# One attention-and-FFN kernel, its commands split into single loads, casts and masks and put in another order

## The chip, the cores and the metric

One core of a Trainium2 chip. The metric is device microseconds of one execution; lower is better. The kernel has 3 runs: 200.95 us median, 199.65 to 203.45. The engines are TensorE (PE in the profile, its weight loads PEld), VectorE (DVE), ScalarE (ACT), GpSimd (POOL) and SyncE (SP, which only issues transfers here). Each runs its own instructions strictly in the order in which the program gives them, and waits for the others by semaphores.

## The reference

Attention over 4 batches, 8 heads, 768 positions, 64 wide, then a maxout FFN on the 3072 tokens:

```python
scores = scale * np.matmul(q, k.transpose(0, 1, 3, 2))
stream_keep = causal & (is_sink | in_win)          # sinks 4, window 64
mask = np.where(retrieval_head, causal, stream_keep)
a = softmax(np.where(mask, scores, -1e9))
x = np.matmul(a, v)            # -> [3072, 512]
h = np.maximum(np.maximum(x @ w1, x @ w2), x @ w3)
out = h @ w_out                # 512 -> 768 -> 512
```

A head is a retrieval head (all of the causal part) or a streaming head (a window and the sinks); which it is comes as data.

## The kernel before

**Units of work.** A batch has two halves of 384 queries. The first half sees 3 key blocks of 128, the second half 6. Heads go in quads of four, that is in two pairs of two heads. An index t counts batch, half and quad: t = 0, 1 are the two quads of batch 0's first half, 2 and 3 of its second half, 4 and 5 of batch 1's first half, up to 15. "Pair 0 to 3" of batch 0 are its four pairs of heads; the first half's third pair is pair 2.

**The steps.** Scores are computed transposed, keys on the partitions: `s t u` (L553) multiplies keys and queries into PSUM for part u of quad t (two parts in a first half, four in a second), and ACT takes the exponential into `pt` (L564). `k t i u e` multiplies a part of `pt` of pair i by a 0/1 mask on engine e (L586). `av t i` multiplies `pt` by the values with a column of ones (L602); DVE takes the reciprocal and scales (L610, L612) into `x`. `x` is turned by a transposing DMA (`av ... D`, L621) or by PE and a copy (`x t i`, L634, L638) into `xT`. Values are cast to f16 into `va` (L504) and, multiplied by a flag of the head, into `vf` (L506); `v t i` does both, one behind the other.

**The FFN.** When a half has its four `xT`, its FFN is put on a queue. Each command `f 1 e` computes one more block of it: one of 18 blocks of four matmuls (L438, 128x384 out of 512), where the first of three is copied out by engine e (L455) and the others are reduced by a maximum on DVE (L458, into `acc` and `hT`), and then three output blocks of six matmuls (L474, copied by engine e, L480). An output block takes two commands, the second of which does nothing. In batch 0's first FFN all blocks of one weight matrix come first, then those of the next.

**Batch 0's queries and keys.** They come by plain DMA in f32 (`hl half pair n`, L187), from SP, keys and queries of n pairs together; are cast to f16 (`cast half pair`, L212, one engine for keys and one for queries); and are turned by six PE transposes and copied into `KQ` (`turnp`, L231, L239). In batch 0's first half the mask is added on PE before the exponential (L537). Later batches come by a casting DMA from POOL (`load b qd`, L251) and are turned on DVE by stream transposes (`turn`, L267). Values come from SP (`load_v b half`, L287), weights by casting DMAs from POOL (`w`, L403, L410).

**What sets the order.** `PROGRAM`, a hand-kept list of 480 commands, is executed in order when the program is built; each command appends its instructions to the engines' queues. No scheduler moves anything. `idle n` issues n matmuls of zeros (L322). Buffers: two score tiles `st` in PSUM, four PSUM banks for all else, five `pt`, three f16 casts each of keys and queries, three value tiles. The letters a, d, p at the end of a command name ACT, DVE and POOL; with two letters, one for each of two instructions.

Of the kernel before, what the change touches and what calls it, by code (L numbers as in the profile page):

```python
# [10 lines left out]
FP16 = mybir.dt.float16  # L11
# [32 lines left out]
FIRST = "hl 0 0 1, ir"  # L44

PROGRAM = (
    "idle 2, idle 8, cast 0 0 aa, hl 0 1 1 ss, hl 0 2 2 ss, read, hl 1 0 2 ss, cast 0 1 pp",
    "flags, cast 0 2 ap, em 1, turnp 0 1 a, far, em 0, turnp 0 0 aa, cast 0 3 da, em 2, em 3",
    "load_v 0 0 4 4, s 0 0 1, s 0 0 0, v 1 1 pp, cast 1 1 pa, turnp 0 3 dd, turnp 0 2 da",
    "w 0 2 0, load_v 0 0 0 4, v 0 0 dp, s 1 0 0, w 0 2 1, s 0 1 0 b, hl 1 2 2 ss, s 1 0 1",  # L50
    "cast 1 2 dp, v 1 0 dd, s 0 1 1, s 1 1 0 b, av 0 0, v 0 1 pp, turnp 1 1 a, s 1 1 1",
    "turnp 1 2 aa, x 0 0 a, s 2 0 1, cast 1 0 dp, load_v 0 1, cast 1 3 ad, av 1 1, s 2 1 1",
    "av 1 0, x 1 1 d, av 0 1, turnp 1 0 ad, s 2 2 1, x 1 0 d, s 3 0 0, m 0, w 1, x 0 1 d",
    "s 2 0 0, m 3, m 1, f 1 d, f 1 d, s 2 1 0, s 2 2 0, m 2, f 1 a, f 1 d, k 2 1 2 p, k 2 0 1 d",
    "w 2, f 1 d, s 2 3 1, load 1 0, w 3, k 3 0 0 d, s 3 1 0, f 1 a, s 2 3 0, load 1 1",
    "k 2 0 3 p, k 2 0 2 p, turnp 1 3 dd, k 3 0 1 p, k 2 1 1 d, k 2 1 3 d, f 1 d, f 1 d",
    "v 2 0 ad, f 1 a, f 1 a, v 3 1 pp, f 1 d, s 3 0 1, v 2 1 dp, s 3 1 1, f 1 a, v 3 0 ap",
    "av 2 0 D, f 1 d, f 1 d, s 3 2 0, turn 1 0 0 0, turn 1 0 0 1, f 1 a, turn 1 0 1 0, s 3 2 1",
    "s 3 3 0, k 3 0 2 p, k 3 1 2 p, turn 1 0 1 1, f 1 a, av 2 1 D, s 3 3 1, k 3 1 1 d",
    "k 3 0 3 p, k 3 1 3 p, f 1 a, k 3 1 0 d, load_v 1 0, gate, f 1 a, s 4 0, k 4 1 0 p",  # L60
    "v 4 0 pp, av 3 0, av 3 1, f 1 a, f 1 a, x 3 0 d, s 4 1, turn 1 1 0 1, x 3 1 a, f 1 d",
    "v 5 1 pp, turn 1 1 1 0, turn 1 1 1 1, turn 1 1 0 0, k 4 0 1 d, k 4 0 0 d, k 4 1 1 p, f 1 a",
    "f 1 a, f 1 d, load_v 1 1, f 1 a, f 1 a, f 1 a, v 4 1 pd, f 1 a, f 1 d, s 5 0, f 1 a, f 1 d",
    "av 4 0 D, k 5 0 0 d, f 1 d, s 5 1, k 5 0 1 p, load_v 2 0, f 1 a, f 1 a, load 2 0, f 1 a",
    "s 6 0, f 1 d, av 4 1 D, f 1 a, v 5 0 ap, f 1 a, s 6 1, f 1 a, av 5 0 D, f 1 d, f 1 d",
    "k 5 1 1 p, k 5 1 0 p, v 7 0 dp, s 6 2, k 6 1 2 p, f 1 a, av 5 1 D, turn 2 0 1 0, f 1 a",
    "v 6 0 ad, s 6 3, turn 2 0 0 1, x 5 1 d, f 1 a, turn 2 0 1 1, load 2 1, load 3 1",
# [12 lines left out]
    "k 10 0 2 p, v 11 1 ap, av 10 0 D, f 1 d, s 11 2, k 11 0 2 p, turn 3 0 0 0, f 1 a",  # L80
    "turn 3 0 0 1, f 1 d, k 11 0 1 d, f 1 a, k 10 1 2 d, f 1 d, v 10 1 ap, f 1 a, turn 3 1 0 1",
    "f 1 a, f 1 a, s 12 0, av 10 1 D, f 1 a, f 1 d, k 12 1 0 p, s 12 1, f 1 d, f 1 a, f 1 a",
    "k 12 0 1 p, turn 3 1 0 0, s 11 3, v 12 1 ad, f 1 a, load_v 3 1, f 1 a, f 1 a, k 11 0 3 d",
    "k 11 1 3 p, f 1 d, f 1 d, k 11 1 1 p, turn 3 1 1 1, f 1 a, f 1 d, av 11 0 D, f 1 d",
    "k 11 1 2 d, f 1 a, k 12 0 0 p, k 12 1 1 d, f 1 a, s 13 0, av 12 0 D, f 1 d, av 11 1 D",
    "k 13 0 0 d, f 1 d, f 1 d, s 13 1, f 1 d, v 15 1 pp, f 1 d, k 13 0 1 p, x 11 1 d, f 1 d",
    "v 15 0 ad, av 12 1 D, k 13 1 1 d, av 13 0 D, s 15 0, f 1 a, f 1 d, f 1 d, f 1 a, f 1 d",
    "f 1 d, f 1 a, k 13 1 0 d, s 15 1, v 14 0 ap, f 1 d, f 1 a, f 1 d, f 1 d, s 14 0, f 1 a",
    "f 1 d, f 1 d, f 1 d, av 13 1 D, s 14 1, f 1 d, x 13 1 d, f 1 d, f 1 d, f 1 a, f 1 a",
    "s 14 2, f 1 a, k 14 1 2 p, v 14 1 ad, k 14 1 1 p, f 1 d, f 1 d, f 1 d, f 1 a, f 1 a",  # L90
    "k 15 0 1 p, s 14 3, f 1 d, k 14 0 3 p, f 1 a, f 1 d, s 15 2, f 1 a, f 1 d, f 1 d, f 1 d",
    "s 15 3, f 1 a, k 15 1 1 d, f 1 a, k 15 1 3 d, f 1 a, k 15 1 2 d, k 14 0 1 p, f 1 a",
    "k 14 0 2 p, k 14 1 3 p, k 15 0 3 d, av 14 0 D, f 1 a, f 1 a, f 1 a, av 14 1 D, f 1 a",
    "f 1 d, k 15 0 2 p, av 15 1 D, f 1 a, av 15 0 D, f 1 d, x 15 1 d, f 1 a, f 1 d, f 1 a",
    "f 1 d, f 1 d, f 1 a, f 1 a, f 1 a, f 1 d, f 1 a, f 1 a, f 1 d, f 1 d, f 1 a, f 1 d, f 1 a",
    "f 1 a, f 1 a, f 1 a, f 1 a, f 1 d, f 1 a, f 1 d, f 1 a, f 1 d, f 1 a, f 1 d, f 1 a, f 1 a",
# [13 lines left out]
def kernel(  # L110
# [68 lines left out]
    def load_pairs(half, hp, n, engines):  # L179
        for nm, src, eng in zip(("ks", "qs"), (k, q), engines):  # L180
            st = (
                pairs2.tile([P, 4, HB, D], FP32, tag=nm, name=nm) if n == 2
                else once.tile([P, 2 * n, HB, D], FP32, name=f"{nm}{hp}")
            )
            m = 2 * n if eng is nc.gpsimd else 2
            for h in range(0, 2 * n, m):
                eng.dma_start(  # L187
                    out=st[:, h : h + m],
                    in_=src[
                        0, 2 * hp + h : 2 * hp + h + m, half * HALF : (half + 1) * HALF  # L190
                    ].rearrange("h (p j) d -> p h j d", p=P),
                )
            for i in range(n):
                staged.setdefault((half, hp + i), []).append(st[:, 2 * i : 2 * i + 2])

    def load_cast(half, hp, n):
        for nm, src in (("kc", k), ("qc", q)):
            st = half16.tile([P, 4, HB, D], FP16, tag=nm, name=nm)
            nc.gpsimd.dma_start(
                out=st[:, 0 : 2 * n],  # L200
                in_=src[
                    0, 2 * hp : 2 * hp + 2 * n, half * HALF : (half + 1) * HALF
                ].rearrange("h (p j) d -> p h j d", p=P),
            )
            for i in range(n):
                cast.setdefault((half, hp + i), []).append(st[:, 2 * i : 2 * i + 2])

    def cast_pair(half, hp, engines):
        cast[half, hp] = []
        for nm, src, op in zip(("kn", "qn"), staged.pop((half, hp)), engines):  # L210
            x = half16.tile([P, HB, 2, D], FP16, tag=nm, name=nm)
            op(out=x, in_=src.rearrange("p h j d -> p j h d"))  # L212
            cast[half, hp].append(x)
# [6 lines left out]
    def turn_pair(half, hp, *engines):  # L220
        if (0, hp // 2) not in KQs:
            KQs[0, hp // 2] = qkt.tile([P, 2, S, 2], FP16, tag="KQ", name="KQ")
        xs = cast.pop((half, hp))
        n = 2 // len(engines)
        for part, op in enumerate(engines):
            tr = bank([P, 1024], FP16, "tr")
            for i in range(n):
                for j in range(HB):
                    c, x = i * HALF + j * P, xs[part + i]
                    if x.shape[1] == HB:  # L230
                        nc.tensor.transpose(  # L231
                            tr[:, c : c + P], x[:, j].rearrange("p h d -> p (h d)"), ident
                        )
# [65 lines left out]
    def load_first(half, hp, n, e="sc"):  # L299
        by = {"s": nc.sync, "c": nc.scalar}  # L300
        load_pairs(half, hp, n, [by[x] for x in e])
# [414 lines left out]
```

## Time and profile before

| | |
|---|---|
| runs shown | 200.95 median, 199.65 to 203.45 us |
| span of the profiled execution | 199.9 us (no other time of it is shown; the median is 1.05 above) |
| PE busy | 190.0 us, 95% |
| DVE busy | 148.3 us, 311 instructions |
| ACT busy | 115.9 us, 171 instructions |
| POOL busy | 90.5 us, 118 instructions |
| first exponential, first FFN product, first output product | 9.85, 23.64, 45.9 us |
| last matmul ends | 196.7 us |

The mean granted clock of TensorE is 0.990; it is 0.50 to 0.72 from 8 to 12 us and 1.00 afterwards. A stretch row of the profile gives, for a window of the span, the busy time of each engine; a busy PE is not the same as a needed PE, since ends of matmuls are modelled. A timeline row gives start, duration, engine, line, operation, and in brackets how long the engine had been idle and what ended that. Durations of neighbours on one engine overlap, so the sum of durations is more than the busy time.

### The profile page before, as it was taken

What the parts mean: (1) busy time and instruction counts of PE and PEld (TensorE: products, weight loads), DVE (VectorE), ACT (ScalarE), POOL (GpSimd) and SP (SyncE); (2) the same over time, 40 slices, a digit from 0 to 9 for tenths busy, and PEclk for the clock granted to TensorE, in tenths of its full rate; (3) what the DMA queues carried; (4) which work ended last, traced back from release to release, by engine and by line L of the source; (5) the groups of instructions that cost most, each with busy time, mean ns of one, the idle gap of its engine ahead of it and who ended that gap; (6) DMA issues with size and microseconds to landing.
All of it is one profiled execution on the core that took longest, in us unless ns stands there. A gap on an engine that the chain in (4) does not pass through costs nothing.

```text
span 199.9 us, 5135 instructions
## 1 busy us (share of the span) xinstructions
PE 190.0 (95%) x2059; PEld 109.3 (55%) x2059; DVE 148.3 (74%) x311; ACT 115.9 (58%) x171; POOL 90.5 (45%) x118
## 2 busy tenths in 40 slices
PE   7688898999999999999999999999999999999993
PEld 2345444565556455666456645574656455765552
DVE  3638965998976789896469998996978288767750
ACT  4489983765658798687776756634366565100011
POOL 3429187583276598490697245652010197000000
PEclk9889999999999999999999999999999999999999
DMA  5999999995979989988521232703500120124004
GB/s 143 312 245 230 196 195 212 208 169 76 283 173 211 162 169 208 218 218 176 147 76 23 43 124 74 159 20 73 167 5 20 53 108 0 23 59 157 3 0 157
DMA packets 48429, 26.48 MB, mean 132 GB/s; under 512 B 36758, under 2 KB 43926, under 8 KB 48406
## 3 DMA queue, kind: packets, MB, share of 16 engines
q1 hardware_dynamic: 43366, 17.96, 37.9%
q0 software_dynamic: 4624, 7.87, 21.9%
q8 instruction: 16, 0.26, 0.6%
q10 hardware_dynamic: 416, 0.33, 0.5%
q14 instruction: 7, 0.06, 0.1%
HBM read 25.17 MB, written 6.29 MB: 157 GB/s over the span
## 4 chain that ended last, share of the span: by engine, by line
PE 75%; DMA 11%; DVE 4%; SPq 3%; issue 2%; ACT 2%; POOL 0%; DVEq 0%
PE yy L438 39%; PE yy L474 14%; PE st L553 9%; PE oacc L602 9%; DMA vs<-in_v_dram 7%; PE yst L438 3%; DMA qs<-in_q_dram 2%; DVE KQ L267 2%; SPq L187 2%; ACT pt L564 1%; DMA xT<-x 1%; PE yst L474 1%; DVE acc L458 1%; DVE hT L458 1%; SPq L621 1%
## 5 line engine op out<-in xcount | busy, mean ns | idle before, releaser
L564 ACT ACTIVATE pt<-st 128x1024 f16<-128x1024 f32 (+3 forms) x98 | 83.3, 905 | 33.0 <-PE st L553 31.0
L586 POOL TENSOR_TENSOR pt<-pt,mk 128x512 f16<-128x512 f16 (+1 forms) x54 | 57.3, 1088 | 38.4 <-ACT pt L564 20.1
L438 PE MATMUL yy<-xT,w1t 128*128 128x384 f16 x180 | 35.8, 327 | 1.2 <-DVE pt L586 1.2
L438 PE MATMUL yy<-xT,w2t 128*128 128x384 f16 x180 | 36.1, 326 | 0.0
L438 PE MATMUL yy<-xT,w0t 128*128 128x384 f16 x180 | 35.8, 327 | 0.3
L458 DVE TENSOR_TENSOR acc<-yy,acc 128x384 f16<-128x384 f32 x45 | 24.8, 557 | 10.7 <-PE yy L438 8.6
L474 PE MATMUL yy<-woutt,hT 128*128 128x512 f16 (+1 forms) x138 | 31.6, 375 | 0.0
L553 PE MATMUL st<-KQ 32*128 32x384 f16 (+5 forms) x560 | 29.4, 281 | 1.4 <-ACT pt L564 0.8
L458 DVE TENSOR_TENSOR hT<-yy,acc 128x384 f16<-128x384 f32 x45 | 24.8, 556 | 4.5 <-PE yy L438 2.3
L602 PEld LDWEIGHTS <-pt 128*128 128x128 f16 x672 | 24.4, 97 | 4.8 <-DVE va L504 0.7
L267 DVE STREAM_TRANSPOSE KQ<-kq 128x384 f32<-128x384 f32 x24 | 25.5, 1132 | 0.6 <-DMA kq<-in_q_dram 0.6
L602 PE MATMUL oacc<-va,pt 128*128 128x65 f16 x352 | 24.9, 193 | 0.5 <-DVE va L504 0.5
L438 PEld LDWEIGHTS <-w1t 128*128 128x128 f16 x192 | 17.5, 98 | 14.1 <-issue 1.6
L438 PEld LDWEIGHTS <-w0t 128*128 128x128 f16 x192 | 17.8, 98 | 13.4 <-issue 0.8
L438 PEld LDWEIGHTS <-w2t 128*128 128x128 f16 x192 | 17.3, 98 | 11.9 <-issue 1.4
L553 PEld LDWEIGHTS <-KQ 32*128 32x128 f16 (+1 forms) x560 | 12.2, 93 | 18.8 <-issue 11.8
L474 PEld LDWEIGHTS <-hT 128*128 128x128 f16 x150 | 13.8, 98 | 14.7 <-issue 0.8
L602 PE MATMUL oacc<-vf,pt 128*128 128x65 f16 x320 | 21.1, 193 | 0.0
L455 ACT CAST acc<-yy 128x384 f16<-128x384 f32 x25 | 12.0, 481 | 13.9 <-PE yy L438 13.5
L612 DVE TENSOR_TENSOR x<-oacc,rc 128x384 f16<-128x384 f32 x32 | 17.8, 557 | 1.1
L480 DVE COPY ot<-yy 128x512 f32<-128x512 f32 (+1 forms) x15 | 10.1, 675 | 9.2 <-PE yy L474 9.2
L506 POOL TENSOR_TENSOR vf<-va,far 128x384 f16<-128x384 f16 x10 | 8.6, 867 | 17.3 <-ACT va L504 12.9
(72 smaller groups left out, 143.4 us busy)
## 6 DMA issues: line engine op xcount, KB each, us to landing
out_dram<-ot SPq DMA_DIRECT2D x23, 256.0 KB, 2.1
vs<-in_v_dram SPq DMA_DIRECT2D x21, 256.0 KB, 5.6
kq<-in_k_dram POOLq DMA_DIRECT2D x6, 384.0 KB, 7.9
kq<-in_q_dram POOLq DMA_DIRECT2D x6, 384.0 KB, 10.0
ks<-in_k_dram SPq DMA_DIRECT2D x8, 192.0 KB, 3.6
qs<-in_q_dram SPq DMA_DIRECT2D x7, 192.0 KB, 4.8
vs<-in_v_dram SPq DMA_DIRECT2D x6, 128.0 KB, 4.8
w0t<-in_moe_w_dram POOLq DMA_DIRECT2D x2, 384.0 KB, 9.4
```

What stands on the lines that cost most here:

```text
L267: nc.vector.transpose(out=dst.rearrange("c (p j) -> c j p", j=n)[:, j0:j1], in_=src.rearrange("c (j i) -> c j i", i=R),)
L438: nc.tensor.matmul(yy[:, 0:HALF], w_t[wi][:, ks, ni * P : (ni + 1) * P], xT[b, half][ks].rearrange("p a t -> p (a t)"), start=(ks == 0), s ...
L455: copy_out[0](out=acc[ni], in_=yy[:, 0:HALF])
L458: nc.vector.tensor_tensor(out=dst, in0=yy[:, 0:HALF], in1=acc[ni], op=ALU.max)
L474: nc.tensor.matmul(yo[:, 0:n], hT[ns][:, tb * P : (tb + 1) * P], woutt[:, ns, c : c + n], start=(ns == 0), stop=(ns == NNB - 1),)
L480: op(out=ot[:, c : c + n], in_=yo[:, 0:n])
L506: vf_engine.tensor_tensor(out=vf[j][:, hs, k0:k1, 0:D], in0=vs[:, hs, 0:1] if half == 0 else va[j][:, hs, k0:k1, 0:D], in1=far[:, hs, k0:k ...
L553: nc.tensor.matmul(sts[g // m][:, g % m, c0 : c0 + n * P], KQ[rows, 0, ki * P : (ki + 1) * P], KQ[rows, 1, t0 : t0 + n * P], start=(c0 == ...
L564: nc.scalar.activation(out=pts[t, i][:, u, h0 : h0 + m, 0:w], in_=st[:, :, 0:w], func=AF.Exp, scale=sc,)
L586: engine.tensor_tensor(out=x, in0=x, in1=m, op=ALU.mult)
L602: nc.tensor.matmul(o[:, qi, hl, 0 : D + 1], pt[:, u, hl, c : c + P], vv[:, 2 * hp + hl, ki, 0 : D + 1], start=(idx == 0), stop=(idx == len ...
L612: nc.vector.tensor_tensor(out=x, in0=o[:, :, :, 0:D], in1=rc.unsqueeze(3).to_broadcast([P, HB, 2, D]), op=ALU.mult,)
```

## The change

Four parts.

1. The commands get finer. `hl` loads keys or queries (a further argument, 0 or 1), `cast` casts one of them, `v` only casts the values and a new `vf` only scales them, and `k` masks one entry of the list (before, the first part of a first half's pair took two mask instructions in one command). The instructions that are issued are the same in number and size, apart from which engine does them and that the zero matmuls and some copies are grouped otherwise.
2. `PROGRAM` is another list, 512 commands. At its start: pair 0 of the first half is cast and turned ahead of the zero matmuls; then come pair 0 of the second half, pair 2 and 3 of the first, pair 1 of both, and scores of the second half stand among those of the first. Weights are issued behind more of POOL's casts.
3. An output block of the FFN takes one command, not two.
4. Helpers that no command used are removed.

```diff
-FIRST = "hl 0 0 1, ir"
 PROGRAM = (
-    "idle 2, idle 8, cast 0 0 aa, hl 0 1 1 ss, hl 0 2 2 ss, read, hl 1 0 2 ss, cast 0 1 pp",
-    "flags, cast 0 2 ap, em 1, turnp 0 1 a, far, em 0, turnp 0 0 aa, cast 0 3 da, em 2, em 3",
-    "load_v 0 0 4 4, s 0 0 1, s 0 0 0, v 1 1 pp, cast 1 1 pa, turnp 0 3 dd, turnp 0 2 da",
-    "w 0 2 0, load_v 0 0 0 4, v 0 0 dp, s 1 0 0, w 0 2 1, s 0 1 0 b, hl 1 2 2 ss, s 1 0 1",
-    "cast 1 2 dp, v 1 0 dd, s 0 1 1, s 1 1 0 b, av 0 0, v 0 1 pp, turnp 1 1 a, s 1 1 1",
-    "turnp 1 2 aa, x 0 0 a, s 2 0 1, cast 1 0 dp, load_v 0 1, cast 1 3 ad, av 1 1, s 2 1 1",
-    "av 1 0, x 1 1 d, av 0 1, turnp 1 0 ad, s 2 2 1, x 1 0 d, s 3 0 0, m 0, w 1, x 0 1 d",
-    "s 2 0 0, m 3, m 1, f 1 d, f 1 d, s 2 1 0, s 2 2 0, m 2, f 1 a, f 1 d, k 2 1 2 p, k 2 0 1 d",
...
+    "cast 0 0 1 a, hl 1 0 2 1 s, hl 0 2 2 1 s, read, hl 1 0 2 0 s, flags, cast 0 0 0 a, em 2",
+    "turnp 0 0 ad, hl 0 2 2 0 s, em 0, em 3, idle 8, far, hl 0 1 1 0 s, hl 0 1 1 1 s",
+    "cast 0 2 1 a, cast 1 0 1 a, s 0 0 0, cast 0 3 1 a, cast 0 2 0 p, cast 1 0 0 d",
+    "load_v 0 0 4 4, idle 2, turnp 1 0 da, s 0 1 0 b, hl 1 2 2 1 s, turnp 0 2 da, cast 0 3 0 p",
+    "cast 0 1 0 d, s 2 0 0, cast 1 1 0 p, hl 1 2 2 0 s, turnp 0 3 dd, cast 1 1 1 d, cast 0 1 1 p",
+    "em 1, s 1 0 0, cast 1 2 1 p, cast 1 2 0 p, v 1 1 p, turnp 0 1 a, turnp 1 1 d, v 1 0 p",
+    "s 1 0 1, vf 1 1 d, s 0 0 1, s 0 1 1, turnp 1 2 dd, s 2 2 0, m 1, vf 1 0 p, cast 1 3 0 d",
+    "s 1 1 1, s 1 1 0 b, m 3, w 0 2 0, load_v 0 0 0 4, w 0 2 1, v 0 0 a, s 2 3 0, cast 1 3 1 p",
+    "vf 0 0 d, s 2 1 0, v 0 1 p, turnp 1 3 dd, av 0 0, av 1 0, vf 0 1 p, av 0 1, s 2 0 1, s 3 0 1",
+    "av 1 1, x 1 0 a, x 0 0 d, s 3 0 0, x 0 1 d, w 1, load_v 0 1, w 2, x 1 1 d, v 2 1 p, load 1 0",
+    "s 2 3 1, f 1 a, s 2 2 1, v 3 0 d, k 2 1 1 d, w 3, m 0, f 1 a, f 1 d, s 3 3 1, s 3 2 1, f 1 d",
+    "s 3 2 0, f 1 d, k 3 1 0 d, f 1 a, k 2 1 2 d, vf 2 1 d, vf 3 0 d, s 2 1 1, s 3 1 1, m 2",
+    "k 3 1 3 p, k 2 0 0 d, f 1 d, f 1 d, k 2 0 2 p, f 1 a, f 1 a, k 2 1 0 p, f 1 d, f 1 a",
+    "k 2 0 1 d, v 2 0 a, f 1 d, v 3 1 a, k 3 1 1 p, vf 2 0 p, f 1 d, turn 1 0 0 1, s 3 3 0",
+    "vf 3 1 p, s 3 1 0, f 1 a, turn 1 0 0 0, f 1 a, k 3 0 0 p, load 1 1, f 1 a, f 1 a",
+    "turn 1 0 1 0, k 3 1 2 p, k 3 0 2 p, turn 1 0 1 1, av 2 0 D, av 2 1 D, load_v 1 0, k 3 0 1 p",
+    "k 3 0 3 p, gate, av 3 1, av 3 0, s 4 0, turn 1 1 0 1, f 1 a, f 1 a, x 3 1 a, k 4 1 0 p",
...
 )
...
-    def load_pairs(half, hp, n, engines):
-        for nm, src, eng in zip(("ks", "qs"), (k, q), engines):
...
+    def load_pairs(half, hp, n, i, eng):
+        nm, src = ("ks", "qs")[i], (k, q)[i]
...
-    def cast_pair(half, hp, engines):
...
+    def cast_pair(half, hp, i, op):
+        nm = ("kn", "qn")[i]
+        x = half16.tile([P, HB, 2, D], FP16, tag=nm, name=nm)
+        op(out=x, in_=staged.pop((half, hp, i)).rearrange("p h j d -> p j h d"))
+        cast[half, hp, i] = x
...
             yield
-            yield
...
-    def prep_v(t, i, op, vf_engine):
...
+    def cast_v(t, i, op):
+        b, half, qd = where(t)
+        k0 = half * HB
+        hs = slice(4 * qd + 2 * i, 4 * qd + 2 * i + 2)
+        op(out=va[b % 2][:, hs, k0 : k0 + HB, 0:D], in_=staged_v[b, half][:, hs])
+
+    def scale_v(t, i, vf_engine):
...
-        for at, u0, nu, cols, n, m0 in APART if t in (3,) else MASKED[half]:
-            if at != u:
-                continue
+        _, u0, nu, cols, n, m0 = (APART if t in (3,) else MASKED[half])[u]
...
-        v=lambda t, i, e: prep_v(int(t), int(i), ops[e[0]], engines[e[1]]),
+        v=lambda t, i, e: cast_v(int(t), int(i), ops[e]),
+        vf=lambda t, i, e: scale_v(int(t), int(i), engines[e]),
```

## The prediction

> **What bounds the kernel now.** I read the busy shares first, then the stretches of the span, then the chain, then the timeline of the first 46 us, instruction by instruction. The first line is the page's busy line; the rest are stretches (time, then busy us and instruction count of PE, PEld, DVE, ACT, POOL, then granted clock, DMA share, GB/s).
>
> ```profile
> PE 190.0 (95%) x2059; PEld 109.3 (55%) x2059; DVE 148.3 (74%) x311; ACT 115.9 (58%) x171; POOL 90.5 (45%) x118
> ...
> 8.50:23.60 15.10, 13.07 (x158) 7.68 (x155) 10.96 (x31) 14.29 (x26) 7.22 (x14) 0.90 1.16 236
> 23.60:45.90 22.30, 20.92 (x251) 12.31 (x252) 17.94 (x40) 14.72 (x19) 15.74 (x18) 1.00 1.07 192
> 45.90:58.00 12.10, 12.10 (x108) 6.45 (x105) 9.94 (x20) 7.59 (x15) 5.19 (x9) 1.00 0.94 192
> 58.00:117.00 59.00, 58.88 (x727) 33.88 (x726) 47.10 (x92) 43.91 (x63) 38.04 (x47) 1.00 0.72 146
> 117.00:180.00 63.00, 63.00 (x699) 36.91 (x698) 48.40 (x97) 29.56 (x42) 21.44 (x21) 1.00 0.26 69
> ...
> 196.70:199.90 3.20, 0.00 (x0) 0.00 (x0) 0.42 (x1) 0.00 (x0) 0.00 (x0) 0.91 0.47 164
> ```
>
> From 45.9 to 196.7 us TensorE has no gap worth naming, and the tail of 3.2 us is the last output. So 150.8 us are a sum of matmuls that the change leaves as they are; time can be won only before 45.9, and lost anywhere. In the head ACT is the full engine up to 23.6 (14.29 of 15.10 us), then nobody is. The timeline says what held the rest:
>
> ```profile
> 9.85 2.00 ACT L564 ACTIVATE pt<-st 128x1024 f16<-128x1024 f32 x2
> ...
> 14.22 3.03 SPq L287 DMA_DIRECT2D vs<-in_v_dram  x3
> ...
> 23.63 1.09 PEld L438 LDWEIGHTS <-w0t 128*128 128x128 f16 x8 [0.43 <-DMA w0t<-in_moe_w_dram]
> ...
> 30.96 1.09 PEld L438 LDWEIGHTS <-w1t 128*128 128x128 f16 x8 [1.39 <-DMA w1t<-in_moe_w_dram]
> ...
> 34.05 0.51 ACT L504 CAST va<-vs 128x384 f16<-128x384 f32 x1 [3.13 <-issue]
> ```
>
> The first exponential starts at 9.85. The first FFN product starts at 23.64, just as its weights land. The second weight matrix holds PE 1.4 us at 31. The second half's values, issued at 14.2 to 17.2, are cast only at 34.05, by ACT and POOL together (POOL at 34.10), so they landed at about 34; the DMA share is above 1 all that time. The first output product (L474) starts at 45.94 in the chain. I use that as the milestone: everything before it in one order is also before it in the other.
>
> **The change part by part.** *1. Up to the first exponential.* The ten zero matmuls that ran at 1.3 to 5.3 us (0.40 us each) now stand eight behind the first pair's transposes and two behind its scores. Casts of pair 0 are on ACT as before (4.0 and 4.4, 0.51 each), so the transposes run at 5.2 to 5.9, the eight zero matmuls to 9.2, the scores to 9.7: first exponential 9.7 against 9.85. No change.
>
> *2. From there to the first FFN product.* ACT is in order and was full, so I add its queue in the new order: nine exponentials of 1024 at 1.0, two of 512 at 0.60, four of 256 at 0.41, one of 768 at 0.81, two casts at 0.52, three KQ or xT copies at 0.50, one of 768 at 0.80: 16.0 us of durations. Neighbours overlap by some 0.04 us (22 of them, 0.9), so 15.1, and the last one, an xT copy, ends at 24.8; with the last xT copy on DVE the first product starts at 25.2, 1.6 later than now. For that, PE by then has done three score steps more (0.3 each) and the last pair's transposes (0.35): 1.25. What could starve ACT there: the loads of the second half's last pairs, which now wait on SP for a cast that ACT does after its first exponential (11.2); with 3.1 to 5.3 us to land they are there at 15 to 17.6, and their transposes are wanted at 17.3. POOL issues the first weights behind two of those casts, two value casts and a scaling (0.51, 0.51, 0.51, 0.51, 0.44): about 17.5 to 19.2 instead of 14.9 to 16.2. They landed in 8.7 to 10.0 us with the queues full; with the second half's values by then mostly in, I take 6: 23.5 and 25, in time. At 10.0 they come at 27.5 and 29.2.
>
> *3. From the first product to the first output product.* PE's work now: 18 blocks at 0.653 (the chain's four-matmul pieces are 0.65) 11.75, eleven score steps 3.3, one transpose 0.35, four AVs at 0.94 3.75, the next batch's first scores 0.6: 19.75 of 22.3 us, 2.55 lost. After: 11.75, eight steps 2.4, 3.75, 0.6: 18.5. Lost there, step by step: PE waits for a score buffer three times (0.3 each, ACT's exponentials being 1.0), and 0.3 to 0.7 where DVE, held behind a mask of scores just computed and two mask builds of 0.7, gives back a PSUM bank late: 1.2. The weight wait goes (the third weight is issued at 21.4 instead of 25.3, and the keys of the next batch's second quad 9 us later than now, behind masks, which takes 0.79 MB, 4 us at 200 GB/s, from in front of the others). So 25.2 + 18.5 + 1.2 = 44.9 against 45.94: -1.0. Bounds: nothing lost, 43.7, -2.2; as much lost as now, 46.25, +0.3.
>
> *4. The long middle.* Casting and scaling of values, and the masks, are placed one by one, and more go to DVE: 8 value casts (0.42), 3 scalings of 384 (0.74) and 4 of 128 (0.35), 9 masks of 512 (0.52) and 2 of 256 (0.28), 3 KQ copies (0.55) and one of 768 (0.80) more; 6 output copies (0.69), 5 acc copies (0.55) and an xT copy (0.35) fewer: +7.4 us. POOL loses about 16. DVE is in order, and behind each of its masks stand the maxima that give back PE's banks. How full does it get? Between the sixth block of the second FFN (58 us now) and the end of the fourth (117) the listed instructions come to 57.8 us of durations before and 64.5 after. DVE overlaps its neighbours, as these rows show (starts 0.38 to 0.48 apart, durations 0.45 to 0.56):
>
> ```profile
> 103.41 0.56 DVE L458 TENSOR_TENSOR acc<-yy,acc 128x384 f16<-128x384 f32 x1
> 103.89 0.45 DVE L586 TENSOR_TENSOR pt<-pt,mk 128x512 f16<-128x512 f16 x1
> 104.27 0.54 DVE L458 TENSOR_TENSOR hT<-yy,acc 128x384 f16<-128x384 f32 x1
> 104.73 0.54 DVE L455 CAST acc<-yy 128x384 f16<-128x384 f32 x1
> ```
>
> so the 57.8 took 47.1 us, and 64.5 will take 52.6 in a stretch of about 58: 90% instead of 80%. That is short of a bound, but the backlog at places (turns of 1.13 us in a row, masks placed right behind their scores) gets longer by about 2 us, and PE has four banks, some 2.6 us of blocks, of tolerance. I charge 1.0; bounds 0 and 5.7 (64.5 against PE's 58.8, if nothing overlapped).
>
> The Trainium skill, page "VectorE: DVE Perf Modes", section "The DRAIN you can't avoid", says that the next Vector operation does not start until the pipe is empty, so that durations add up; by it the middle would cost 5.7 and not 1.0. The rows above speak against it here: the mask starts 0.48 behind a maximum of 0.56.
>
> *5. Loads of later batches.* The next load of keys and queries stands behind three masks on POOL (1.17 each) and so some 3 us later after its scores; it took 8.85 us to DVE's turn now (59.58 to 68.43), where DVE waited 0.59. In the new order the turn comes about 11.5 us after those scores, the keys about 12.7: DVE waits 1 us more, mostly inside PE's tolerance: +0.2 (0 to 1). Removing the second empty yield of each output block changes no instruction. The tail is the same chain: the last AV, 3.9 us of output products over its transposing DMA (2.3), the last FFN: 0.
>
> Sum: -1.0 + 1.0 + 0.2 = +0.2, on the profiled execution's 199.9: 200.1. The runs shown have their median, 200.95, 1.05 above that span, so 201.2 on their scale. Own range of this case: 199 to 204.
>
> **The rivals.** *A, slower: DVE becomes the bound.* It decides from the point where DVE has no idle time left between 58 and 117 us: with 97% or more, each wait of its own (for an exponential, a load) is handed to PE. Price: the upper bound above, 5.7 instead of 1.0: 204.8 on the span, 205.9 on the runs' scale; with its own idle waits up to 208. For it: the work, and masks set 0 to 1.3 us of PE time behind their scores, where an exponential pair takes 2. Against: 47.1 us measured for 57.8 listed.
>
> *B, slower or level: the first weights are late.* At 10.0 us to landing the first product starts at 27.5 to 29.2 instead of 25.2, and the milestone, with the same work behind it, comes 2.3 to 4.0 later: 203.5 to 205.2 on the runs' scale. For it: the weights are behind five POOL instructions that wait for loads themselves. Against: the value loads that kept the queues full are in front of them by then.
>
> *C, faster: the head gains more.* If the first product starts as early as now, 23.64, because ACT's queue runs tighter than I add it up, and nothing is lost in step 3, the milestone is 23.64 + 18.5 = 42.1, -3.8; with a middle as dense as now that is 196.1 on the span, 197.2 on the runs' scale, give or take 1. For it: the waits for the values (34.05) and the second weight disappear. Against: ACT's sum, which no order shortens.
>
> **How the numbers follow.** The forecast 0.38, A 0.26, B 0.14, C 0.22. Two per cent, about what a measurement of this kernel can tell from no change, are 4.0 us: 196.9 and 205.0. Faster by more: half of C and a little of the forecast's spread, 0.11 + 0.04 = 0.15. Slower by more: nearly all of A, half of B, a little of the forecast, 0.25 + 0.07 + 0.04 = 0.36. Between: 0.49. The range takes in C down to its middle and A but for its end: 197 to 207.5.
>
> **What would show it.** Right: first product (L438's successor) at 24.5 to 26 us, first output product at 44 to 46, no weight wait at the second matrix, DVE 51 to 54 us busy in the stretch that ends with the fourth FFN, PE gaps there of 2 us at most. Step 2 is wrong if ACT has gaps between 10 and 25 us that end with a KQ copy; step 3 if PE's longest wait before 45 us is for a weight; step 4 if PE waits for DVE (maxima, output copies) in the middle for more than 3 us, or not at all. The forecast as a whole is wrong if the middle stays as dense as now and the head is 4 us shorter, or if PE loses more after 46 us than the head can give.

## The result, and the profile after

| | before | after |
|---|---|---|
| runs | 200.5 us median of 4 (199.65 to 203.45) | 224.19 us median of 4 (221.03 to 225.76) |
| ratio of the runs | | 1.1055, 95% interval 1.0946 to 1.1165 |
| span of the profiled execution | 199.9 | 219.3 |
| first exponential, first FFN product, first output product | 9.85, 23.64, 45.9 | 10.02, 25.87, 48.46 |

The change costs 10.6%. Here and below a time is the median of all runs of a kernel and a ratio is taken from its fast runs alone, so the two need not agree (224.19/200.5 is 1.118). Of the 19.4 us between the two spans only 2.5 arise before the first output product, the milestone of the prediction (2.7 where both starts are read from the timeline, which has 45.77 for before). The busy line of the profile after:

```profile
PE 191.6 (87%) x2059; PEld 109.3 (50%) x2059; DVE 156.2 (71%) x329; ACT 115.9 (53%) x171; POOL 76.3 (35%) x100
```

PE's work is the same, its share fell from 95% to 87%. The stretches say where (columns as before: time, then busy us and count of PE, PEld, DVE, ACT, POOL, then granted clock, DMA share, GB/s):

```profile
8.50:25.87 17.37, 14.87 (x183) 8.97 (x182) 13.27 (x32) 14.69 (x23) 11.19 (x21) 1.00 1.10 222
25.87:48.46 22.59, 19.52 (x239) 11.77 (x237) 19.96 (x35) 10.36 (x15) 11.93 (x13) 1.00 0.92 169
48.46:75.69 27.23, 27.07 (x273) 14.25 (x270) 21.40 (x48) 19.77 (x30) 12.44 (x14) 1.00 0.80 169
75.69:84.50 8.81, 0.00 (x1) 0.00 (x0) 0.00 (x0) 0.90 (x1) 4.17 (x6) 0.59 1.02 188
84.50:90.00 5.50, 5.50 (x37) 2.79 (x37) 4.20 (x7) 1.01 (x2) 0.00 (x0) 0.73 1.19 263
90.00:108.00 18.00, 17.07 (x258) 10.54 (x256) 15.47 (x29) 13.11 (x20) 12.35 (x16) 1.00 0.48 88
108.00:131.00 23.00, 20.13 (x194) 10.79 (x195) 19.19 (x43) 11.30 (x17) 7.23 (x8) 1.00 0.43 99
131.00:154.00 23.00, 23.00 (x292) 13.79 (x281) 19.90 (x39) 13.62 (x20) 5.11 (x5) 1.00 0.17 51
154.00:170.00 16.00, 14.89 (x161) 7.86 (x160) 10.46 (x22) 9.68 (x14) 5.76 (x6) 1.00 0.23 70
```

For 8.81 us in the middle PE and DVE do nothing at all; behind that PE runs at half clock up to 87.5, which costs 3 us of work at half speed, 1.5. The long dense middle of before is now interrupted at 90 to 131 (3.8 us idle) and 154 to 170 (1.1) too. PE's waits (line, what it waited for, total, times, longest) name two kinds of cause:

```profile
PE yy L411 <- DMA xT<-x: 11.3, 4, 8.8
PE yy L411 <- DVE acc L431: 2.4, 2, 2.0
PE oacc L576 <- DVE vf L482: 1.3, 2, 0.9
PE oacc L576 <- DVE acc L431: 0.9, 1, 0.9
```

Before, PE never waited for an `xT`. L411 is the FFN product (L438 before), L595 the transposing DMA (L621 before), L233 the casting load of keys and queries (L251), L269 the load of values (L287), L560 the masks (L586), L482 the scaling of values (L506). L474 is the cast of values (L504; the L474 of before is the output product, now L447), L431 the maximum (L458), L576 the product with the values (L602), L584 and L586 the reciprocal and the scaling into `x` (L610, L612), L529 the scores (L553), and L362 builds masks.

The longest wait is for the fourth `xT` of the third FFN. PE's row, then SP's own queue and POOL's issues around it (timeline of after: start, duration, engine, line; in brackets the idle time and what ended it):

```profile
84.50 0.48 PE L411 MATMUL yy<-xT,w0t 128*128 128x384 f16 x1 [8.81 <-DMA xT<-x]
...
64.19 4.76 SPq L269 DMA_DIRECT2D vs<-in_v_dram  x3
69.04 3.84 SPq L595 DMA_TRANSPOSE xT<-x  x1
72.98 1.19 SPq L595 DMA_TRANSPOSE xT<-x  x1
74.26 0.53 SPq L454 DMA_DIRECT2D out_dram<-ot  x1
74.89 1.21 SPq L595 DMA_TRANSPOSE xT<-x  x1
...
74.57 0.60 POOL L233 DMA_DIRECT2D kq<-in_k_dram  x1
75.16 0.54 POOL L233 DMA_DIRECT2D kq<-in_q_dram  x1
75.70 1.17 POOL L560 TENSOR_TENSOR pt<-pt,mk 128x512 f16<-128x512 f16 x1
76.80 0.59 POOL L233 DMA_DIRECT2D kq<-in_k_dram  x1
77.39 0.54 POOL L233 DMA_DIRECT2D kq<-in_q_dram  x1
```

`x` of that pair was ready at 71.84 (DVE's row 71.28 plus 0.56). SP, in order, reached its transpose only at 74.89: it had issued without a pause from 64.19 on, and one transpose in front had held it for 3.84 us (1.2 is usual) while the values in front of that one, issued at 65.37, were still landing. And then the transfer took 9.58 us to land, where the median of the transposes is 2.4:

```profile
65.37 8.35 DMA vs<-in_v_dram
...
74.89 9.58 DMA xT<-x
```

These are pieces of the chain. (The chain puts the issue at 74.89 down to a value cast that DVE ended at 74.86; but SP was issuing until 74.79, and in experiment 2 the transpose goes out as soon as SP is free and `x` is there.) The trace's single DMA records show what happened in those 9.58 us. Counted per microsecond of the span, with the mean duration of one record: the 3072-byte rows of POOL's four loads, and the 256-byte rows on SP's queue, which are the transpose's 384 rows, 24 for each of 16 DMA engines:

```
span us   3072 B rows, us each    256 B rows, us each
76-77        17  0.78                 0
77-78        41  0.27                25  0.031
78-79        58  0.25                60  0.031
79-80        63  0.25                75  0.028
80-81        63  0.25                64  0.031
81-82        62  0.25                79  0.028
82-83        63  0.25                61  0.028
83-84        54  0.27                20  0.030
```

In every full microsecond from 78 to 83 there are about as many small rows as large ones, as if they were taken in turn; the records don't show the order on one engine. 24 rounds of 0.25 + 0.03 us are 6.7 us for a transfer whose rows are served in about 1 us when nothing lies beside them. The loads `load 2 1` and `load 3 0`, which the new order puts right behind `x 5 1`, lie beside it. The Trainium skill, page "DMA: Bandwidth & Descriptors", section "Queues, rings and completion order", says that each DMA engine goes round its queues and takes a whole packet, typically 9 to 17 descriptors, from one before it turns to the next. The equal counts agree with the going round; how many rows one turn takes the table doesn't show.

### The profile page after: what moved, and what is told of

It is laid out like the page before. It is cut to its first block, busy times and chain, and to the rows that moved or that the text cites. A ratio compares the mean times of both kernels' runs of the same rounds, so it can differ in the third digit from the quotient of the medians.

```text
span 219.3 us, 5146 instructions
## 1 busy us (share of the span) xinstructions
PE 191.6 (87%) x2059; PEld 109.3 (50%) x2059; DVE 156.2 (71%) x329; ACT 115.9 (53%) x171; POOL 76.3 (35%) x100
## 4 chain that ended last, share of the span: by engine, by line
PE 53%; DVE 20%; DMA 15%; issue 6%; ACT 3%; SPq 1%; DVEq 0%; ACTq 0%
PE yy L411 26%; PE yy L447 8%; DMA xT<-x 8%; DMA vs<-in_v_dram 6%; PE oacc L576 6%; PE st L529 6%; DVE acc L431 4%; DVE KQ L249 3%; PE yst L411 3%; DVE x L586 2%; DVE pt L560 2%; DVE hT L431 2%; DVE vf L482 2%; ACT pt L540 2%; DMA qs<-in_q_dram 2%
## 5 line engine op out<-in xcount | busy, mean ns | idle before, releaser
L560 POOL TENSOR_TENSOR pt<-pt,mk 128x512 f16<-128x512 f16 (+1 forms) x43 | 48.1, 1131 | 97.7 <-ACT pt L540 70.8
L411 PE MATMUL yy<-xT,w0t 128*128 128x384 f16 x180 | 36.9, 328 | 11.4 <-DMA xT<-x 11.3
L411 PE MATMUL yy<-xT,w1t 128*128 128x384 f16 x180 | 36.2, 331 | 2.0 <-DVE acc L431 2.0
L411 PE MATMUL yy<-xT,w2t 128*128 128x384 f16 x180 | 36.4, 331 | 0.8 <-DVE acc L431 0.4
L431 DVE TENSOR_TENSOR acc<-yy,acc 128x384 f16<-128x384 f32 x45 | 24.2, 551 | 13.0 <-PE yy L411 5.2
L428 ACT CAST acc<-yy 128x384 f16<-128x384 f32 x31 | 15.1, 486 | 34.3 <-PE yy L411 34.1
L447 PE MATMUL yy<-woutt,hT 128*128 128x512 f16 (+1 forms) x138 | 31.7, 375 | 0.0
L411 PEld LDWEIGHTS <-w1t 128*128 128x128 f16 x192 | 17.8, 98 | 24.1 <-issue 13.6
L529 PE MATMUL st<-KQ 32*128 32x384 f16 (+4 forms) x560 | 28.7, 279 | 0.3 <-DVE KQ L221 0.2
L431 DVE TENSOR_TENSOR hT<-yy,acc 128x384 f16<-128x384 f32 x45 | 24.7, 557 | 4.7 <-PE yy L411 2.8
L576 PEld LDWEIGHTS <-pt 128*128 128x128 f16 x672 | 24.1, 97 | 7.4 <-issue 4.2
L411 PEld LDWEIGHTS <-w0t 128*128 128x128 f16 x192 | 17.6, 98 | 16.1 <-issue 5.1
L576 PE MATMUL oacc<-va,pt 128*128 128x65 f16 x352 | 24.8, 193 | 0.2 <-DVE pt L560 0.2
L411 PEld LDWEIGHTS <-w2t 128*128 128x128 f16 x192 | 17.7, 99 | 13.9 <-issue 2.7
L560 DVE TENSOR_TENSOR pt<-pt,mk 128x512 f16<-128x512 f16 (+1 forms) x43 | 22.0, 523 | 2.7 <-ACT pt L540 2.7
L576 PE MATMUL oacc<-vf,pt 128*128 128x65 f16 x320 | 20.8, 193 | 3.0 <-DVE vf L482 1.3
L447 PEld LDWEIGHTS <-hT 128*128 128x128 f16 x150 | 13.8, 98 | 14.9 <-issue 0.7
L529 PEld LDWEIGHTS <-KQ 32*128 32x128 f16 (+1 forms) x560 | 12.1, 93 | 18.0 <-issue 12.7
L586 DVE TENSOR_TENSOR x<-oacc,rc 128x384 f16<-128x384 f32 x32 | 17.8, 557 | 1.1
L428 DVE CAST acc<-yy 128x384 f16<-128x384 f32 x14 | 7.6, 553 | 11.7 <-PE yy L411 11.6
```

The costliest lines, as they stand in the source:

```text
L411: nc.tensor.matmul(yy[:, 0:HALF], w_t[wi][:, ks, ni * P : (ni + 1) * P], xT[b, half][ks].rearrange("p a t -> p (a t)"), start=(ks == 0), s ...
L428: copy_out[0](out=acc[ni], in_=yy[:, 0:HALF])
L431: nc.vector.tensor_tensor(out=dst, in0=yy[:, 0:HALF], in1=acc[ni], op=ALU.max)
L447: nc.tensor.matmul(yo[:, 0:n], hT[ns][:, tb * P : (tb + 1) * P], woutt[:, ns, c : c + n], start=(ns == 0), stop=(ns == NNB - 1),)
L529: nc.tensor.matmul(sts[g // m][:, g % m, c0 : c0 + n * P], KQ[rows, 0, ki * P : (ki + 1) * P], KQ[rows, 1, t0 : t0 + n * P], start=(c0 == ...
L560: engine.tensor_tensor(out=x, in0=x, in1=m, op=ALU.mult)
```

## The experiments

Two theories for the middle were put against each other first. *P (packets)*: POOL's loads take every other place on the DMA engines. *Q*: SP's queue order alone makes the transposes late. Rival *D* is rival A of the prediction, DVE as the bound. Diffs show commands of `PROGRAM`; "..." is left out.

**1. The loads behind the next mask and scaling on POOL** (e1_kq_late).

```diff
-"s 6 2, k 6 1 1 p, k 6 1 0 d, x 5 1 d, f 1 d, load 2 1, f 1 a, k 6 0 1 p, s 7 0, load 3 0",
-"... turn 2 0 1 0, f 1 a, vf 6 1 p, k 6 1 2 p, f 1 d",
+"s 6 2, k 6 1 1 p, k 6 1 0 d, x 5 1 d, f 1 d, f 1 a, k 6 0 1 p, s 7 0",
+"... turn 2 0 1 0, f 1 a, vf 6 1 p, load 2 1, load 3 0, k 6 1 2 p, f 1 d",
```

> The changed order, with the two loads of keys and queries that POOL issues at 74.57 and 76.80 us (load 2 1, load 3 0) put behind the mask and the scaling that follow them on POOL; nothing else moves. Theory P (packets): the fourth transposing DMA of the third FFN took 9.58 us to land because its 24 packets per DMA engine alternate one by one with the 3 KB packets of those loads (0.25 us each); without them it lands in 2.4 us, PE's wait of 8.8 us at 75.7 becomes 1.5, the half clock behind it goes too: span 219.3 - 7.3 - 1.6 = 210.4, time about 4% lower than that of the changed kernel (ratio to before 1.06). Theory Q (SP's queue is what is late, whatever POOL loads): the transpose is still issued at 74.9 and still late, span 218 to 220, ratio 1.10. Theory D (VectorE is the bound, rival A of the prediction): PE's wait moves to VectorE's rows, span 217 to 219.

Measured: 214.19 us, ratio 1.0738 (1.0686 to 1.0790), span 212.9. PE's row for the same product, and POOL's first load (timeline):

```profile
77.38 0.32 PE L411 MATMUL yy<-xT,w0t 128*128 128x384 f16 x1 [1.58 <-DMA xT<-x]
...
77.03 0.60 POOL L233 DMA_DIRECT2D kq<-in_k_dram  x1
```

The transpose is issued at 74.98, as late as in the changed kernel, and lands 2.4 us later: a load that comes 2.5 us later is worth 7.2 us of waiting. Q alone is out. The span fell by 6.4 and not 8.9: this execution has two stretches of half clock that the other had not (37.1 to 40.5, behind a wait of 2.0 us that both have, and 105.3 to 108.7, at the fourth FFN).

**2. The values out of SP's way** (e2_v_early).

```diff
-"s 5 1, k 4 0 2 p, k 4 0 0 p, load_v 1 1, f 1 a, v 5 0 a, ...",
-"k 5 0 2 p, f 1 a, f 1 a, load_v 2 1, av 4 1 D, ...",
+"s 5 1, k 4 0 2 p, k 4 0 0 p, load_v 1 1, load_v 2 1, f 1 a, v 5 0 a, ...",
+"k 5 0 2 p, f 1 a, f 1 a, av 4 1 D, ...",
```

> The changed order, with the values of the third batch's second half (load_v 2 1) issued right behind load_v 1 1, ahead of the third FFN's transposes on SP, instead of between them; nothing else moves, POOL's loads least of all. Theory P: SP is then not held at 69.04 (3.84 us), the fourth transpose is issued at about 72 instead of 74.89, ahead of POOL's load of 74.57, and lands in 2.4 us: no wait of PE there, span 219.3 - 8.8 - 1.6 = 209. Theory Q expects the same of this run (and differs in e1_kq_late). Theory D: 217 to 219. If only the load on POOL counted and the issue time not, the transpose would still land at 84 and nothing would change.

Measured: 211.84 us, ratio 1.0593 (1.0538 to 1.0648), span 210.8. SP's rows:

```profile
63.46 7.97 SPq L595 DMA_TRANSPOSE xT<-x  x3
72.62 1.18 SPq L595 DMA_TRANSPOSE xT<-x  x1
```

The fourth transpose goes out at 72.62 instead of 74.89, ahead of POOL's load (75.32 here), and the third FFN starts without a wait. So both matter: SP's order made the transpose late, and late meant beside POOL's rows, where it took four times as long. What is left is the fourth FFN:

```profile
102.79 0.80 PE L411 MATMUL yy<-xT,w0t 128*128 128x384 f16 x2 [1.50 <-DMA xT<-x]
```

**3. The same collision put into the kernel before** (e3_before_kq_early).

```diff
-"k 5 1 1 p, k 5 1 0 p, v 7 0 dp, s 6 2, k 6 1 2 p, f 1 a, av 5 1 D, turn 2 0 1 0, f 1 a",
-"v 6 0 ad, s 6 3, turn 2 0 0 1, x 5 1 d, f 1 a, turn 2 0 1 1, load 2 1, load 3 1",
+"k 5 1 1 p, k 5 1 0 p, load 2 1, load 3 1, v 7 0 dp, s 6 2, k 6 1 2 p, f 1 a, av 5 1 D, ...",
+"v 6 0 ad, s 6 3, turn 2 0 0 1, x 5 1 d, f 1 a, turn 2 0 1 1",
```

> The kernel before, with one edit: load 2 1 and load 3 1 are issued ahead of the casting and scaling of values 7 0 (about 63.5 to 66 us instead of 68.9 to 71.1), so that their packets lie beside the third FFN's last two transposing DMAs (issued 64.99 and 67.87). Theory P: these take 6 to 9 us to land instead of 2.3; the last is wanted at 72.3 and comes at 75 to 77: PE waits 3 to 5 us, span 203 to 205 against 199.9, ratio 1.015 to 1.025. Theory Q and theory D: SP's order and VectorE's work are as before, nothing changes, ratio 1.00.

Measured: 209.63 us, ratio 1.0503 (1.0443 to 1.0563), span 207.5. Two loads issued some 4 us earlier, nothing else, cost the kernel before half of what the whole change costs. PE's rows in the timeline, and the landing of the transposes by the group of `xT`:

```profile
76.45 0.32 PE L438 MATMUL yy<-xT,w0t 128*128 128x384 f16 x1 [2.84 <-DMA xT<-x]
78.79 0.83 PE L438 MATMUL yy<-xT,w0t 128*128 128x384 f16 x2 [2.02 <-DMA xT<-x]
```

```profile
DMA to landing us min/median/max: 2.3/2.4/12.5
```

The sign and the mechanism were expected, the size was not: both transposes were late, 4.9 us together, 3.4 us of half clock followed (78.1 to 81.5, 1.7 us), and this execution waited 1.8 us for the first weights besides.

**4 and 5. Head and middle exchanged** (hyb_after_head, hyb_before_head). The first of this pair takes the changed order up to the 18th block of the first FFN and the rest from the kernel before; the second is its mirror.

```diff
 # hyb_after_head
 "cast 0 0 1 a, ... f 1 a, f 1 a"   (133 commands of the changed order)
+what is left of the order of before, on the engines of before
```

> The changed order up to the 18th block of the first FFN (its first 133 commands), then what is left in the order and on the engines of the kernel before. If the loss of 19.4 us splits as the spans say (2.5 us up to the first output product, the rest behind), and the rest is made by the new order of the middle: about 199.9 + 2.5 = 202.4 (201 to 204), ratio 1.01. If a late head were what pushes the middle into its waits: 210 or more.

Measured: 205.98 us, ratio 1.0321 (1.0268 to 1.0373), span 203.2.

> The mirror of hyb_after_head: the commands of the kernel before up to the 18th block of the first FFN, then what is left in the changed order and on its engines. If head and middle add up (head +3.3 by hyb_after_head's span of 203.2, the rest 16): span 216 (213 to 218), ratio 1.08. If the two only do harm together, because the changed head ends its work late: span about 200 to 205.

Measured: 219.56 us, ratio 1.0855 (1.0715 to 1.0995), span 216.7. The two parts add up within their intervals: 3.2% and 8.6% against 10.6% for both, 3.3 and 16.8 us on the spans against 19.4. The two scales differ because the span of 199.9 is a long one for the kernel before: beside runs 1 to 4 it had 197.4 to 199.0, so differences from 199.9 come out 1 to 2.5 us too small. With the new head and the old middle PE is busy 59.74 of the 60 us from 50 to 110, so a late head doesn't push the middle into its waits:

```profile
50.00:110.00 60.00, 59.74 (x688) 33.77 (x687) 47.15 (x88) 43.59 (x65) 37.82 (x49) 1.00 0.82 173
```

**6. The whole way of the transposes cleared** (e5_middle_mended).

```diff
 # the edits of 1 and 2, and:
-"load 3 1, v 8 0 d, load_v 3 1, s 8 0, f 1 a, k 7 0 0 d, k 7 0 1 p, av 6 1 D, v 8 1 p, f 1 a",
-"s 8 1, f 1 d, av 7 1 D, v 9 1 p, s 10 0, x 7 1 d, vf 7 0 p, av 7 0 D, v 10 1 d, ...",
+"load 3 1, v 8 0 d, s 8 0, f 1 a, k 7 0 0 d, k 7 0 1 p, vf 7 0 p, av 6 1 D, av 7 0 D, av 7 1 D,",
+"v 8 1 p, f 1 a, s 8 1, f 1 d, v 9 1 p, s 10 0, x 7 1 d, load_v 3 1, v 10 1 d, ...",
```

> The changed order with the transposing DMAs' way cleared, nothing else: load 2 1 and load 3 0 behind the next mask and scaling on POOL (as in e1_kq_late), load_v 2 1 behind load_v 1 1 (as in e2_v_early), load_v 3 1 behind the fourth FFN's last transpose instead of between its transposes, and av 7 0, av 7 1 with vf 7 0 pulled right behind av 6 1. Theory P with SP's order: the third FFN has no wait (as in e2_v_early, 210.8), the fourth's waits of 2.8 us and the half clock behind them go too: span 210.8 - 2.8 - 1.5 = 206.5 (205 to 208), ratio 1.03 to 1.04. If the fourth FFN's wait is not from the values in front on SP, 210.

Measured: 209.36 us, ratio 1.0474 (1.0414 to 1.0535), span 207.0; PE waits for no `xT` any more. So the transposes' way is 1.1055 - 1.0474 = 5.8 points of the 10.6, the head 3.2, and 1.5 are left (0.7 to 2.3 by the intervals of runs 4 and 6). DVE is now busy 53.21 of the 59 us from 58 to 117, and PE 56.41. What PE waits for in the middle is DVE:

```profile
PE oacc L576 <- DVE vf L482: 1.3, 2, 0.9
PE oacc L576 <- DVE pt L560: 1.0, 2, 0.8
```

**7 and 8. The engines alone** (e7_engines_only, e10_engines_no_casts). The order of before, with the engines of the changed kernel from the second batch on.

```diff
 # for example
-"v 4 0 p, vf 4 0 p, ... k 4 0 0 d, k 4 0 1 d"
+"v 4 0 d, vf 4 0 p, ... k 4 0 0 p, k 4 0 1 d"
```

> The order of the kernel before, command for command, but from the second batch on each mask, value cast, scaling, xT copy, acc copy and output copy runs on the engine that the changed kernel gives it (88 commands changed). This is the prediction's step 4 by itself: DVE's work as in the changed kernel, its order of transfers not. Step 4 as predicted: +1.0 (0 to 5.7) on 199.9, ratio 1.005. Rival A (VectorE as the bound): 204 to 206, ratio 1.03. Theory P: POOL's loads shift only by what its masks in front shift them, 199.5 to 202.

Measured: 219.34 us, ratio 1.0998 (1.0916 to 1.1079), span 217.8. No theory had this. PE's longest wait and DVE's row in front of it say why:

```profile
53.73 0.50 PE L608 MATMUL tr<-ident,x 128*128 128x128 f16 x3 [8.11 <-DVE x L586]
...
52.62 0.36 DVE L474 CAST va<-vs 128x384 f16<-128x384 f32 x1 [8.61 <-DMA vs<-in_v_dram]
```

In the order of before the value cast `v 4 0` comes early, which is harmless on POOL. On DVE it waits 8.61 us for its load, and the scaling into `x`, whose result PE turns next, stands behind it: PE idle 8.1 us, and half clock from 49.5 to 59.8. The new order had moved that cast behind more work together with its engine. So this run doesn't measure step 4; the next one leaves the casts and the `xT` copies where they were.

> e7_engines_only without the value casts and xT copies: the order of the kernel before, and from the second batch on only masks, scalings, acc copies and output copies on the engines that the changed kernel gives them (69 commands). The wait of 8.1 us at 45.6, for a copy behind a value cast that waits for its load on DVE, should be gone with its half clock (217.8 - 8.1 - 1.5 = 208 as a lower bound of what else changed). Rival A (DVE as the bound in the middle): DVE's waits between 80 and 130 stay, span 204 to 208. Step 4 as predicted: 200 to 202.

Measured: 208.82 us, ratio 1.0333 (1.0238 to 1.0428). 3.3% are 6.7 us, without a new order of transfers. That is near rival A's price, but not by rival A's cause. DVE has 12 masks and 5 scalings more than in the kernel before and 10 copies fewer (they went to ACT), so its sum is the same, 148.6 us for 148.3; between 58 and 117 it is busy 47.84 us, for 47.10. PE waits for single masks instead (its waits, total, times, longest):

```profile
PE oacc L576 <- DVE pt L560: 2.4, 4, 1.6
```

So which engine does which piece at which place costs time, with no more work in sum. These waits are less than the 6.7; the profiled execution (span 208.6) also waits 2.5 for the last weight, and where the rest arises the run doesn't settle.

**9. The head on one engine** (e8_head_one_engine). In the changed kernel DVE was busy 10.00 of the 10 us from 31 to 41, but not with more instructions (15; in the kernel before 16 took 7.79): some took long. DVE's rows in the timeline of after, and POOL's at the same time:

```profile
33.24 1.91 DVE L362 TENSOR_SCALAR mk<-kept,least 128x512 f16<-128x512 f16 x2
35.08 1.04 DVE L560 TENSOR_TENSOR pt<-pt,mk 128x512 f16<-128x512 f16 x1
38.83 2.27 DVE L560 TENSOR_TENSOR pt<-pt,mk 128x512 f16<-128x512 f16 x1
...
32.92 2.09 POOL L560 TENSOR_TENSOR pt<-pt,mk 128x512 f16<-128x512 f16 x2 [1.03 <-ACT pt L540]
34.97 1.84 POOL L482 TENSOR_TENSOR vf<-va,far 128x384 f16<-128x384 f16 x2
38.52 2.29 POOL L560 TENSOR_TENSOR pt<-pt,mk 128x512 f16<-128x512 f16 x2
```

A mask takes DVE 0.42 by the median; here it lasts as long as POOL's work beside it. So eleven of POOL's operations in the head were given to DVE, on the kernel of run 4:

```diff
-"k 3 1 3 p, ... k 2 0 2 p, ... k 2 1 0 p, ... k 3 1 1 p, vf 2 0 p, ... vf 3 1 p, ... k 3 0 0 p",
+"k 3 1 3 d, ... k 2 0 2 d, ... k 2 1 0 d, ... k 3 1 1 d, vf 2 0 d, ... vf 3 1 d, ... k 3 0 0 d",
 # and k 3 0 1, k 3 0 2, k 3 1 2, k 3 0 3
```

> hyb_after_head (span 203.2), with the nine masks and two scalings that POOL does for the first batch's second half (pairs of t 2 and 3) given to DVE. That adds 4.4 us to DVE (6 of 0.42, 3 of 0.28, 2 of 0.55) where it is fullest. Theory S (sum: DVE is simply full there): the first output product comes 3 to 4 us later, span 206 to 207.5. Theory L (lock: DVE's operations from SBUF to SBUF are held for as long as a POOL operation runs beside them, 1.24 and 0.75 instead of 0.35, 1.05 and 2.27 instead of 0.42, some 3 to 4 us in all between 31 and 41): without POOL's work they shrink to 0.35 to 0.55, the two nearly cancel, span 202.5 to 204.5.

Measured: 207.68 us, ratio 1.0398 (1.0328 to 1.0468), span 204.2. The profiled execution lies where theory L put it, but it is the fastest of five: the others have spans of 205.7 to 206.4, about the lower end of theory S, and the ratio is no better than the 1.0321 of run 4. So the time decides nothing; the rows do. The same two DVE rows:

```profile
31.96 0.61 DVE L362 TENSOR_SCALAR mk<-kept,least 128x512 f16<-128x512 f16 x2
32.49 0.75 DVE L560 TENSOR_TENSOR pt<-pt,mk 128x512 f16<-128x512 f16 x2
```

Two mask builds take 0.61 instead of 1.91, and each mask 0.42. PE's wait of 2.0 us is gone, and it ends the first FFN's products at 39.7, against 42.4 in run 4 (0.6 of that because they begin earlier, at 25.10 for 25.72), although DVE has 4.4 us more to do. The gain is then lost in one wait:

```profile
46.65 1.04 PE L529 MATMUL st<-KQ 32*128 32x384 f16 x16 [3.56 <-DVE rc L584]
```

The next batch's scores wait for DVE's stream transposes, which end at 46.5 and 46.6 in the two kernels (the bracket names the reciprocal that ends at the same moment). DVE operations that read PSUM show no such stretching (0.55 for a maximum, with or without POOL beside it). The Trainium skill, page "SBUF — State Buffer", section "SBUF: two separate sides", has the rule: a DVE operation in a two-port mode or with two SBUF inputs shares a pair of ports with GpSimd, and the one that comes second waits for the whole instruction of the first. The rows of both kernels agree, and go further: the mask of 2.27 us begins at 38.83 and ends at 41.10, behind both of POOL's masks (38.52 to 40.81) and not behind the first.

**10. Outputs in front of that wait** (e9_outputs_first).

```diff
-"load_v 1 0, gate, s 4 0, k 4 1 0 p, ... av 3 1, f 1 a, x 3 0 d, s 4 1, turn 1 1 0 1, x 3 1 a, f 1 d",
+"load_v 1 0, gate, f 1 a, f 1 a, s 4 0, k 4 1 0 p, ... av 3 1, f 1 a, x 3 0 d, s 4 1, turn 1 1 0 1, x 3 1 a",
```

> e8_head_one_engine (span 204.2) with two of the first FFN's three output blocks (1.29 us each, copied out by ACT) ahead of the next batch's first scores (s 4 0) instead of behind the third quad's outputs. In e8_head_one_engine PE had everything of the first FFN done some 3 us earlier than in hyb_after_head, and then waited 3.56 us for DVE's four stream transposes in front of those scores, and ran 3.4 us at half clock. If that is where the gain went: the wait is filled with 2.6 us of output products, the half clock goes: span 204.2 - 2.6 - 1.5 = 200 (199 to 202), ratio 1.00 to 1.015. If DVE's sum up to the first products of the second FFN is the bound whatever PE does: 203 to 204.

Measured: 205.94 us, ratio 1.0299 (1.0233 to 1.0365), span 204.1. The wait shrank from 3.56 to 0.97, and the half clock is gone. The spans of the two profiled executions hide what this gave, since that of run 9 was its fastest: the median time fell by 1.7 us, 1.0 point, at the edge of the noise. In the profile the last matmul ends at 199.96, for 201.04 in run 9, although the first FFN begins 1.3 us later (26.39 for 25.10); the tail behind it happens to be longer. So some 2.4 of the expected 4.1 was gained. The second FFN begins at 52.75, for 54.98, and its fourth chunk waits 0.78 for a copy; DVE is busy 7.31 of the 7.4 us from 41 to 48.4. By the span this is nearer to the second expectation; that DVE's sum holds the rest is argued, not shown. No version here beats the kernel before.

## Why the prediction was wrong, by its own steps

The forecast was 201.2 (197.0 to 207.5), the time 224.19. The step that failed is **5, loads of later batches**, with its sentence on the tail beside it. It priced a load by one question, whether DVE's stream transposes would get their keys in time, and a transposing DMA by one number, 2.3. It charged 0.2 (0 to 1). It did not ask what a load does to the transfers that lie beside it. Runs 1, 2, 3 and 6 show that: 5.8 points of 10.6, some 12 us. It followed the loads through POOL's queue, and did not look at what stands in front of the transposes on SP's.

Step 5 is not the only one that failed. With the transposes' way cleared (run 6) the time is still 209.36, outside the range. The larger part of that is the head, for which **step 3** charged -1.0 (bounds -2.2 to +0.3): it came out at +2.5 at the milestone and at 3.2% of the time in run 4, so its sign was wrong too.

Two readings of before would have shown the danger. Its transposes took up to 5.5 us to land, so something could stretch them. And the two lists give the PE work between the last AV of a half and the first product of its FFN, worked out from the rows (0.65 a block, 1.29 an output block, 0.57 or 0.34 a score step): for the third to seventh FFN 4.8, 5.7, 7.3, 5.5 and 7.6 us before, and 3.7, 4.4, 5.0, 4.8 and 6.1 after. Into that cover go the reciprocal and scaling, SP's queue and the landing of 2.3. The change took 0.7 to 2.3 us from each, and put loads of keys and queries into the third's and a load of values into the fourth's.

**Step 1** was right (10.02 for 9.7). **Step 2** was right in time and reason: 25.87 for 25.2, ACT at work but for one gap of 1.12 us in front of scores, weights issued at 18.2 to 19.8, landed in 7.0 to 8.0 (6 taken) and in time. **Step 3** was mis-sized beyond its bounds: from there to the milestone 22.6 us instead of 19.7, 19.5 of them work (18.5 listed) and 3.1 lost (1.2 charged). I had put the loss down to waits for PSUM banks behind masks, which is where it shows (2.0 us for a maximum), but the masks were slow because POOL was at work beside them; run 9 shows that. **Step 4**: DVE's total came as added up (156.2 for 148.3 + 7.4). In the mended order (run 6) what is left for it is about 1.5 points, 3 us, inside 0 to 5.7 and above the 1.0 charged; there DVE is busy 53.21 us from 58 to 117, where the prediction had 52.6, and PE is idle for 2.6, where it allowed 2. In the order of before the new engines for masks, scalings and copies cost 6.7 (run 8), with no more work for DVE in sum, so the sum that step 4 went by is not what sets the price there. Durations did not add up even in run 9's fullest stretch (two maxima in 1.01, 0.55 each). The prediction took only half of what the Trainium skill, page "VectorE: DVE Perf Modes", section "The DRAIN you can't avoid", says: it goes on that a next operation that is not held starts earlier, and the overlapping rows agree with that half.

**The rivals.** A had a true part, since PE waits for DVE in the head and in runs 6 and 8. But its condition, 97% between 58 and 117, was not met: DVE was busy 40.71 of the 59 us in the changed kernel (69%) and 53.21 in run 6 (90%). B did not happen. C was excluded by the first product. None named the transposes. What the prediction gave as its own refutation did happen: PE lost more after 46 us than the head can give.

Of the 19.4 us on the spans, 2.5 are the head, 8.8 the one wait, 1.5 the half clock behind it, and 5.1 the other idle time of PE between the milestone and the tail. The last 1.5 are not assigned: they lie in stretches that count as busy.

## What to carry to other kernels

For each transfer that PE's next work needs, write down when it is issued, what stands in front of it on its queue, and which loads with large rows lie beside it on other queues: its landing time is a property of its neighbours. When commands are reordered, compare the cover of every hand-over, one by one, and not only the sums of the engines. An operation changes its engine only together with its place: a cast that waits for a load is harmless where nobody stands behind it.

## What the runs showed of the hardware that was not expected

- A transposing DMA of 96 KB lands in 2.3 to 2.4 us, in 9.6 beside loads with rows of 3 KB, and in up to 12.5 where three transposes stand one behind the other beside such loads (run 3).
- SP is held too while issuing: a transpose's issue took 3.84 us instead of 1.2 while values issued in front of it were still landing.
- A wait of PE of 2.0 us can be followed by half clock or not. It was in runs 1, 2 and 6 (3.4 us each, 37.1 to 40.5 in run 1), and not in the profile of after nor in run 4, where the same wait was as long. With the 8.8 us wait of after came 10.2 us (77.2 to 87.5). The Trainium skill, page "TensorE: Matmul & The Clock Gate", section "What's actually happening", gives a window of 3413 ns that runs freely: 3.4 and three times 3.4 agree with that. The gap after which the clock drops was shorter here than a whole window. That a wait is followed by half clock in one execution and not in another may be why the runs of the changed kernel spread over 4.7 us; no run tests that.
- DVE's masks and mask builds last as long as POOL's work beside them: 2.27 for 0.42 at the worst, through two POOL operations. Maxima, which read PSUM, keep their 0.55.
